# Lightning attention followed by a SiLU feed-forward layer on one core: four units as one group, scores ahead of outputs, and a new list

## The chip, the cores and the metric

The kernel runs on one core of a Trainium2 chip. The metric is device time in microseconds for one execution of the whole program. The core has five engines that run at the same time, each through its own list of instructions: PE (TensorE, the matmuls; its weight loads are shown apart as PEld), DVE (VectorE), ACT (ScalarE), POOL (GpSimd) and SP (SyncE, which here only issues DMAs). They wait for each other through semaphores. Matmuls read SBUF and write PSUM, which has eight banks of 128 partitions by 512 float32 values; DVE, ACT and POOL empty the banks.

## What is computed

```python
# q, k, v: 4 x 8 x 768 x 64 (batch, heads, positions, head size), lam: one rate per head; block = 64
for b in range(nb):                                    # 12 blocks in a row of the batch
    qb, kb, vb = (x[:, :, sl] for x in (q, k, v))      # sl: the 64 positions of block b
    intra = (einsum('bhic,bhjc->bhij', qb, kb) * Dmask) @ vb       # Dmask: lam ** (i - j), lower triangle
    inter = einsum('bhid,bhde->bhie', qb * lam_pow, kv_state)
    out[:, :, sl] = intra + inter
    kv_state = lam_block * kv_state + einsum('bhsd,bhse->bhde', kb * rev_pow, vb)
x = out.transpose(0, 2, 1, 3).reshape(3072, 512)       # 3072 tokens, 8 heads of 64
h = x @ w_in                                           # first product, 512 x 2048
return (h / (1 + exp(-h))) @ w_out                     # SiLU, second product, 2048 x 512
```

## The kernel before

**Tiles.** The 3072 tokens are cut into 24 *units* of 128. Two units form a *pair* (256 positions of one row of the batch); there are 12 pairs, three to a row. All matmuls run on bf16 operands and accumulate in PSUM.

**What happens to a pair n.** Its q, k and v are loaded (one DMA of 512 KB each on SP's queue), cast to bf16 and put in order (`cast`, L407 on ACT, L409 on DVE, L411 on POOL), v being multiplied by its decay at the same time (`scale`, L414, which gives `vd`). Keys and queries are then transposed into `kqT`: on TensorE for pairs 0 to 3, and by a transposing DMA on SP's queue for the others; there are three buffers `kqT`. Then comes the pair's *burst* on TensorE. From pair 3 on one burst holds, for the new pair n, the products that make the *states* (k against v, L659, 64 columns each) and the *scores* (k against q, L670, 128 columns each), and for the pair before, n-1, the *inter* products (the state against q, L633, which `CROSSED` pairs 4 to 11 use, and L617 for pair 3) and the *outputs* (masked scores against v, L626). Two half arrays of 64 rows are used, row 0 and row 1; the steps of a burst are made as two lists, one for each row, and these are merged by the time that each list has used so far. The order of the parts within a row is written out by hand at the end of `burst`. The inter products and the outputs of a unit accumulate into one bank; since both row halves of the array write there, a `fence` (an empty instruction on TensorE that waits for the last inter product) stands ahead of the first output.

After the burst DVE multiplies the scores by the triangle (`mask`, L414, giving `st`), and multiplies the outputs by their decay (`xt`, L414, 128x512 in bf16), which is the input of the first product. The states go through a chain: `y` (L789, DVE, the sum with the carried state), `xf` (L414, the decayed sum, on DVE or POOL), and two `xe` (copies to bf16 in `xs_all`, L407 or L411). The inter products of the next burst need these copies. So each burst waits for the masks and the copies of the pair ahead of it and for the transposed `kqT` of the new pair.

**First product** (`product1`, L935): x times w_in for a *group* of units, 16 slices of 128 columns of w_in by four slices of 128 rows. A group of two units has 256 columns for each matmul, a group of four has 512. ScalarE applies SiLU to each full bank (L951) and writes `g`. The groups of units 16 to 23 use a scheme of seven products in place of eight (`product1_of_four`, matmuls L1254) with sums of w_in and of x (`wsum`, `xsum`) and copies between the products (`to u`, `u2`, `u3`, and the sums `h22`, `h12`).

**Second product**: g times w_out. Units 0 to 11 take 16 matmuls of 512 columns each (`product2`, L977). The groups of units 12 to 23 take the scheme of seven products (`product2_of_four`, L1126). It needs sums of quarters of w_out (`bsum`, five of them, by m = 5, 1, 2, 7 and 6) and sums of g (`asum`). A sum is made by DVE or POOL (L1017), or by DMA: a copy on SP's queue and then an accumulating DMA on POOL's queue that adds the second operand. `MOVED` names the groups whose `asum` go by DMA (the lines L1107 and L1113 issue them), `BMOVED` the `bsum` that do.

**The opening** waits for the loads. TensorE runs filler matmuls on a tile of ones (L1321) until about 19 us. Each result goes out from `osb` by a DMA, mostly on ACT's queue.

**What sets the order.** All work is a list of tasks, each with a key (its due place), a cost on each engine that may take it, what it depends on, and the buffers that it holds. A list scheduler (`Planner.order`) plays the tasks through with these costs and pools of buffers (`POOLS`) and so fixes, before the program is built, on which engine and in which place of that engine's list every task stands. `SHIFT` adds to the key of named tasks, and `HOME` fixes the engine of named tasks. On the chip each engine runs its list in that order, so a task that is late holds up whatever stands behind it on its engine. `xt2` and `xt4` are the pools of `xt` for groups of two and of four units; eight banks are shared by all (four from the start, and the four of `st2` and `xd` once the first pairs are done).

Of the kernel before, what the change touches and what calls it, by code (L numbers as in the profile page):

```python
# [39 lines left out]
def names_of(tag):  # L40


    if not isinstance(tag, tuple):
        return tag, None, None
    kind, n = tag[:2]
    if kind in ("cast", "scale", "burst", "mask", "y", "xe", "xf", "xt"):
        whole = "pair", n
    elif kind in ("first", "silu", "x", "to u", "u2", "u3", "h12", "h22"):
        whole = "group", n
    elif kind in ("seven", "a", "a copy", "to P", "to B", "to R", "on R", "m3", "c11", "c12", "c21", "c22"):  # L50
        whole = "four", n
    else:
        whole = None
    return tag, tag[:2] if len(tag) > 2 else None, whole


class Planner:
# [5 lines left out]
    BEGIN = {"PE": 0.8, "ACT": 5.6, "DVE": 2.7, "POOL": 3.4, "SP": 0.8}  # L63
    SWITCH = 0.095

    SHIFT = {('cast', 10, 1, 0): -0.5, ('cast', 10, 1, 1): -2.5, ('cast', 6): -3.5, ('cast', 7, 1, 0): -1.5, ('first', 2): -0.5,
             ('first', 2, 6): -8, ('first', 3, 6): -8.5, ('first', 4, 4): 1, ('first', 5, 0): -4, ('first', 5, 6): -0.5,
             ('first', 6): 6.25, ('first', 6, 11): 2.25, ('first', 6, 12): -1, ('first', 6, 14): 13.25, ('first', 6, 15): 2.25,
             ('first', 6, 2): 0.5, ('first', 6, 3): 0.25, ('first', 6, 4): -4.5, ('first', 6, 5): -10.75, ('first', 7): -0.25,
             ('first', 7, 0, 4): 1.75, ('first', 7, 1, 4): 1, ('first', 7, 2, 3): 1, ('first', 8, 0, 5): -4,  # L70
             ('first', 8, 1, 1): -3.5, ('first', 8, 2, 4): 4.5, ('four', 12): 4.5, ('four', 20): -0.75, ('group', 2): 0.25,
             ('group', 3): -5.5, ('group', 7): 4.75, ('group', 8): -7.5, ('load w', 3, 1): -1.5, ('mask', 11): 5.75, ('mask', 5): 3,
             ('mask', 7, 0, 1): 3, ('mask', 8, 0, 0): 5.75, ('mask', 9, 0, 1): 0.25, ('outputs', 0, 0): 4, ('pair', 10): 2.5,
             ('pair', 11): -9.75, ('pair', 4): -7.5, ('pair', 5): -0.75, ('pair', 9): 8.75, ('scale', 3, 0): -1, ('score', 1): 8,
             ('second', 10): 7, ('seven', 12): 0.5, ('seven', 12, 3): -8.25, ('seven', 12, 5): -4.75, ('seven', 16): 3.75,
             ('seven', 20): 3.75, ('silu', 8, 1, 0, 1): 2.75, ('states', 2, 0): 6.75, ('store', 9): -2, ('turn', 3, 0, 1): -10.75,
             ('turned', 1): -7.25, ('u3', 8): 5.5, ('w', 1): 6.75, ('xe', 0, 0, 1): 4.5, ('xe', 11): 11.75, ('xe', 3, 0, 0): 1.5,
             ('xf', 6): -10.25, ('xt', 7, 1): 7, ('y', 10, 0, 0): 5.75}
    HOME = {('a', 16, 1, 1): 'POOL', ('a', 20, 5, 0): 'POOL', ('a', 20, 5, 1): 'POOL', ('b', 3, 1): 'POOL',
            ('cast', 11, 1, 1): 'POOL', ('cast', 3, 0, 1): 'ACT', ('cast', 4, 0, 0): 'DVE', ('cast', 5, 0, 0): 'POOL',  # L80
            ('cast', 5, 1, 0): 'POOL', ('cast', 5, 1, 1): 'ACT', ('cast', 6, 0, 0): 'DVE', ('cast', 6, 1, 0): 'DVE',
            ('cast', 6, 1, 1): 'ACT', ('cast', 7, 1, 0): 'DVE', ('cast', 7, 1, 1): 'ACT', ('cast', 8, 1, 1): 'DVE',
            ('cast', 9, 0, 0): 'POOL', ('cast', 9, 1, 0): 'POOL', ('cast o', 1, 1): 'DVE', ('cast o', 2, 0): 'ACT',
            ('cast o', 2, 1): 'ACT', ('cast w', 1, 3): 'POOL', ('m3', 12): 'DVE', ('result', 1): 'ACT', ('scale', 11, 0): 'POOL',
            ('scale', 9, 0): 'POOL', ('to u', 7, 3): 'DVE', ('turned', 0, 0, 1): 'DVE', ('turned', 0, 1, 0): 'ACT',
# [3 lines left out]
    FIRST, LAST, AHEAD = {"SP": 1.15, "ACT": 1.15, "POOL": 1.0}, 1.0, 0.75  # L89

    def __init__(self, pools, becomes):
# [194 lines left out]
def kernel(  # L286
# [15 lines left out]
    NU = B * S // U  # L302
    NP = H // 2
# [3 lines left out]
    EARLY = 4  # L307
    FINE = (0,)
    TIED, SOLO, CROSSED = 3, (3,), range(4, 12)
    AWAY, XAWAY, OWN = range(5,12), (), (0, 1)  # L310
    PORT = 3
    SMALL = (0, 1)
    OKEY = 0.0
    WKEY, WCAST, WON = -2.0, {"POOL": 0.75, "ACT": 0.62, "DVE": 0.45}, [("POOL", "ACT", "DVE")] * 2 + [("POOL", "DVE"), ("POOL", "ACT")]
    FIRST_ONES, ONES_UNTIL = 10, 19.0
    BMOVED, POOLED = (), (6,)
    LOADED, MOVED, HEAD = (4, 9), (12,16), (1.8, 1.8, 1.2, 0.6)
    TKEY, SEVENS, LAG, WSKEY, FIRST_SEVENS = 9.0, 12, 5.0, 14.0, (16,20)

    ctx.enter_context(tc.manual_schedule())  # L320
    const = ctx.enter_context(tc.tile_pool(name="const", bufs=1))
# [281 lines left out]
    def burst(n, alone=False):  # L603
# [3 lines left out]
        o, new = dict(last_pair), n < NU // 2 and not alone  # L607
# [38 lines left out]
        if new:  # L646
            kq, kqT, vd, ck, cv, turned, kq_of, t_of = ready_of[n]
# [28 lines left out]
        def queue(row, what, width, fn, *more, part=slice(None)):  # L676
            rows[row].extend([(what, 0.0005 + 0.00044 * width, lambda a=(k, r) + more: fn(*a), k) for k, r in steps][part])
# [52 lines left out]
    def attention(n):  # L730
# [593 lines left out]
    ends, first = {}, {}  # L1324
# [61 lines left out]
```

## Time and profile before

| | before |
|---|---|
| three runs, us | 204.65, 205.16, 205.41 (median 205.16) |
| the profiled execution, us | 204.5 |
| its span, first to last instruction, us | 202.8 |
| granted TensorE clock, share of full speed | 0.998 |
| bytes moved by DMA | 44.43 MB, mean 219 GB/s |

All times are those of one core. The profile is one execution; `span` runs from its first to its last instruction, and the rest of its own time lies around that. A busy share is the time that an engine worked over the span. In the rows of a view, a line such as `PE banks L935 x40` is a run of 40 instructions of line 935 on TensorE that write `banks`; `out<-in` gives the tiles with their partitions by elements and type, and `x16` a count. In the timeline the first column is the start in us from the span's start and the second how long the run of instructions lasted until the last of them ended. Matmuls overlap: the next one starts before the last has ended, so for a pace one takes the distance of starts. The list of waits has rows `waiting <- released by: us, times, longest`. The rows of DMA queues give issues, KB each and the median us from issue to landing; those of issuing instructions give the least, the median and the longest issue in ns.

### The profile page before, as it was taken

The page shows a single profiled execution, that of the slowest core. Times are in us where ns is not written, and L with a number is a line of the kernel's source. Part 1 is how long each engine was busy: PE and PEld are TensorE (multiplying, and loading weights), DVE is VectorE, ACT ScalarE, POOL GpSimd, SP SyncE. Part 2 cuts the span into 40 slices and gives each one's busy share as a digit, 9 for nine tenths or more (in the row PEclk, how much of TensorE's full clock was granted, in tenths as well). Part 3 has the DMA queues.
Part 4 walks back from the last instruction along what each step waited for, and adds up shares of the span by engine and source line. Part 5 has one row for each costly group of instructions (what it writes and reads, how often), then busy time and mean ns, then how long its engine had stood idle before and what let it go on. Part 6 is the DMA issues. An engine that isn't in the chain of part 4 may idle for free.

```text
span 202.8 us, 6082 instructions
## 1 busy us (share of the span) xinstructions
PE 196.8 (97%) x2585; PEld 145.3 (72%) x2585; DVE 146.2 (72%) x231; ACT 123.4 (61%) x193; POOL 71.4 (35%) x84
## 2 busy tenths in 40 slices
PE   6999999999999999999999999999999999999993
PEld 2776887867865557557776465458888888888882
DVE  3697749778994949599795875969765766743972
ACT  3697887849785655705384626683796878564010
POOL 4105430222560400058766041338954372000800
PEclk9999999999999999999999999999999999999999
DMA  4999999999999999899999471119997967111324
GB/s 110 339 335 366 386 362 334 368 313 382 230 282 261 318 344 298 208 311 218 303 255 213 130 128 33 57 58 222 176 184 184 218 179 136 52 55 52 107 103 155
DMA packets 71658, 44.43 MB, mean 219 GB/s; under 512 B 18448, under 2 KB 64528, under 8 KB 71632
## 3 DMA queue, kind: packets, MB, share of 16 engines
q1 hardware_dynamic: 62400, 34.74, 62.4%
q0 software_dynamic: 5456, 4.46, 14.4%
q10 hardware_dynamic: 3776, 4.86, 7.2%
q8 instruction: 20, 0.33, 0.6%
q14 instruction: 6, 0.05, 0.1%
HBM read 27.27 MB, written 6.29 MB: 165 GB/s over the span
## 4 chain that ended last, share of the span: by engine, by line
PE 90%; DVE 5%; issue 2%; ACT 1%; ACTq 0%
PE banks L935 27%; PE banks L1126 18%; PE banks L977 17%; PE banks L1254 12%; PE banks L1321 4%; PE banks L626 2%; PE banks L670 2%; PE banks L578 2%; DVE kq L409 1%; DVE xt L414 1%; PE banks L633 1%; DVE st L414 1%; PE banks L659 1%; PE banks L848 1%; PE banks L898 1%
## 5 line engine op out<-in xcount | busy, mean ns | idle before, releaser
L935 PE MATMUL banks<-xt,w_in_bf 128*128 128x256 bf16 (+1 forms) x448 | 67.4, 288 | 0.4 <-DVE xt L414 0.2
L951 ACT ACTIVATE g<-banks 128x512 bf16<-128x512 f32 x64 | 46.0, 745 | 26.8 <-PE banks L935 25.4
L935 PEld LDWEIGHTS <-w_in_bf 128*128 128x128 bf16 x448 | 42.9, 98 | 15.3 <-issue 0.8
L977 PE MATMUL banks<-w_out_bf,g 128*128 128x512 bf16 x192 | 49.6, 379 | 0.0
L414 DVE TENSOR_TENSOR st<-banks,tri 128x512 bf16<-128x512 f32 (+1 forms) x42 | 29.9, 757 | 3.7 <-PE banks L670 2.9
L977 PEld LDWEIGHTS <-g 128*128 128x128 bf16 x192 | 18.3, 98 | 19.1
L414 DVE TENSOR_TENSOR xt<-banks,lam_xe 128x512 bf16<-128x512 f32 x24 | 16.0, 684 | 12.5 <-PE banks L626 12.3
L1126 PE MATMUL banks<-bsum,g 128*128 128x256 bf16 x160 | 21.2, 273 | 0.0
L407 ACT ACTIVATE kq<-raw 64x512 bf16<-64x512 f32 (+3 forms) x24 | 18.5, 799 | 2.7 <-DMA raw<-in_k_dram 1.2
L407 ACT ACTIVATE osb<-banks 128x512 f32<-128x512 f32 (+1 forms) x15 | 8.7, 582 | 17.5 <-PE banks L977 12.2
L1126 PEld LDWEIGHTS <-asum 128*128 128x128 bf16 x176 | 17.2, 98 | 2.0
L409 DVE CAST kq<-raw 64x512 bf16<-64x512 f32 (+3 forms) x21 | 15.2, 741 | 4.0 <-DMA raw<-in_k_dram 2.5
L1126 PEld LDWEIGHTS <-g 128*128 128x128 bf16 x160 | 15.6, 98 | 1.9
L414 POOL TENSOR_TENSOR xf<-y,lam_be 128x256 f32<-128x256 f32 (+1 forms) x11 | 8.2, 749 | 22.1 <-DVE y L789 21.9
L1017 DVE TENSOR_TENSOR asum<-g 128x1024 bf16<-128x1024 bf16 x11 | 9.1, 836 | 8.3 <-PE banks L1126 2.9
L1270 ACT ACTIVATE g<-tmp 128x512 bf16<-128x512 f32 x16 | 12.4, 774 | 3.5 <-DVE tmp L1017 3.3
L1017 DVE TENSOR_TENSOR tmp<-banks,tmp 128x512 f32<-128x512 f32 x16 | 11.0, 687 | 4.8 <-PE banks L1254 4.1
L414 DVE TENSOR_TENSOR vd<-raw,lam_v 128x1024 bf16<-128x1024 f32 (+1 forms) x11 | 12.3, 1120 | 3.0 <-DMA raw<-in_v_dram 2.9
L1254 PE MATMUL banks<-xsum,wsum 128*128 128x256 bf16 x96 | 14.4, 273 | 0.0
L1017 POOL TENSOR_TENSOR asum<-g 128x1024 bf16<-128x1024 bf16 x3 | 6.4, 2121 | 22.8 <-PE banks L1126 19.1
L1254 PEld LDWEIGHTS <-wsum 128*128 128x128 bf16 x128 | 12.4, 98 | 1.5
L1321 PE MATMUL banks<-ones 128*128 128x128 bf16 (+1 forms) x85 | 11.0, 277 | 1.9 <-DVE ones L358 1.5
(96 smaller groups left out, 294.6 us busy)
## 6 DMA issues: line engine op xcount, KB each, us to landing
raw<-in_k_dram SPq DMA_DIRECT2D x11, 512.0 KB, 5.4
raw<-in_q_dram SPq DMA_DIRECT2D x11, 512.0 KB, 6.1
raw<-in_v_dram SPq DMA_DIRECT2D x11, 512.0 KB, 7.6
out_dram<-osb ACTq DMA_DIRECT2D x18, 256.0 KB, 3.6
raw_w<-in_moe_w_in_dram SPq DMA_DIRECT2D x8, 512.0 KB, 8.0
raw_w<-in_moe_w_out_dram SPq DMA_DIRECT2D x8, 512.0 KB, 6.6
asum<-g SPq DMA_DIRECT2D x8, 256.0 KB, 2.6
asum<-g POOLq DMA_DIRECT2D x8, 256.0 KB, 5.1
```

Of the source, the lines that this page charges most:

```text
L407: nc.scalar.activation(o, i, AF.Copy)
L409: nc.vector.tensor_copy(o, i)
L414: (nc.vector if e == "DVE" else nc.gpsimd).tensor_tensor(o, a, b, op=AL.mult)
L578: nc.tensor.transpose(t[:, r, m, :], kq_of()[:, i, r, 2 * m:2 * m + 2, :], ident)
L935: nc.tensor.matmul(t[:, j, :], lhsT=w_in_bf[:, ko, 128 * m:128 * m + 128], rhs=xt[gi].tile[:, ko, :], start=(ko == 0), stop=(ko == KI - 1))
L951: nc.scalar.activation(t.rearrange("p j (c a r) -> p (j c) r a", c=n // U, r=2), psum_of(bank).rearrange("p (jc r a) -> p jc r a", r=2, a= ...
L977: nc.tensor.matmul(psum_of(bank), lhsT=gs[gi, ko][1](1, 128 * gp, 128)[:, 0], rhs=w_out_bf[:, ko], start=(ko == 0), stop=(ko == KO - 1))
L1017: (nc.vector if e == "DVE" else nc.gpsimd).tensor_tensor(o, x, y, op=op)
L1126: nc.tensor.matmul(part(bank, u), lhsT=lhs(u), rhs=b_of(ko), stop=ko == 7, skip_group_check=True, start=opens and not ko and not u)
L1254: nc.tensor.matmul(two_of(bank)[:, f], lhsT=(wb[0].tile if wb else w_quarter(*wl))[:, ko, fs], rhs=(xsum(xr) if isinstance(xr, int) else x ...
L1270: nc.scalar.activation(t.rearrange("p j (c a r) -> p (j c) r a", c=2, r=2), src().rearrange("p (jc r a) -> p jc r a", r=2, a=64), AF.Silu)
L1321: nc.tensor.matmul((t if b.pool == "bank" else t[:, 0])[:, 0:w], lhsT=ones[:, 0:128], rhs=ones[:, 0:w], start=True, stop=True)
```

## The change

Four things are changed. (1) Units 8 to 11 form one group of four where they were two groups of two, and the pools of `xt` go from four and two buffers to two and three. (2) In a burst of a new pair that also holds the outputs of a pair in `CROSSED` (4 to 11), row 0 gets two steps of scores ahead of its outputs (it had none) and row 1 six (it had four); the rest of the scores still follow the outputs. A step is two matmuls. (3) The sums of w_out with m = 1, 7 and 6 go by DMA (`BMOVED`). (4) `SHIFT` and `HOME` are replaced as a whole, so that the scheduler gives a new list. In `SHIFT`, `HOME` and the spelling of four lines nothing else is touched.

```diff
-    SHIFT = {('cast', 10, 1, 0): -0.5, ('cast', 10, 1, 1): -2.5, ('cast', 6): -3.5, ('cast', 7, 1, 0): -1.5, ('first', 2): -0.5,
...
-            ('xf', 10, 0, 1): 'POOL', ('xf', 4, 0, 1): 'DVE', ('xf', 7, 0, 0): 'POOL'}
+    SHIFT = {('cast', 11, 1, 0): -0.5, ('cast', 5, 0, 1): 2, ('cast', 7, 1, 0): 7, ('cast o', 2, 0): -5, ('first', 2, 3): 1.5,
...
+             ('xe', 9, 0, 0): -3, ('xf', 6): -1.5, ('y', 10, 0, 0): -3.5, ('y', 6): -2.5, ('y', 8, 0, 0): -2}
+    HOME = {('a', 20, 2, 1): 'POOL', ('b', 4, 0): 'POOL', ('cast', 10, 1, 0): 'DVE', ('cast', 11, 0, 0): 'ACT',
...
+            ('xe', 6, 0, 0): 'POOL'}
...
-    BMOVED, POOLED = (), (6,)
+    BMOVED, POOLED = (1, 7, 6), (6,)
...
-                 xt2=4, xt4=2, g=7, osb=4, one=3, two=2, set=2)
+                 xt2=2, xt4=3, g=7, osb=4, one=3, two=2, set=2)
...
-    groups = [[0, 1], [2, 3], [4, 5], [6, 7], [8, 9], [10, 11]] + [list(range(4 * n, 4 * n + 4)) for n in range(3, NU // 4)]
+    groups = [[0, 1], [2, 3], [4, 5], [6, 7], ] + [list(range(4 * n, 4 * n + 4)) for n in range(2, NU // 4)]
...
-            ahead = NP if new and o["n"] in CROSSED else 0
+            ahead = (2, NP + 2) if new and o["n"] in CROSSED else (0, 0)
             if new:
-                queue(1, "s", 128, score, 1, part=slice(ahead))
+                queue(0, "s", 128, score, 0, part=slice(ahead[0]))
+                queue(1, "s", 128, score, 1, part=slice(ahead[1]))
             queue(0, "o", 128, output, 0)
             queue(1, "o", 128, output, 1)
...
-            queue(0, "s", 128, score, 0)
+            queue(0, "s", 128, score, 0, part=slice(ahead[0] if o else 0, None))
             if o:
-                queue(1, "s", 128, score, 1, part=slice(ahead, None))
+                queue(1, "s", 128, score, 1, part=slice(ahead[1], None))
```

The code that `BMOVED` chooses is in the kernel before as well; for a sum named there it issues the copy on SP and the addition on POOL:

```python
t = add((TKEY + i / 4 - 2, 0), {"SP": 0.55}, put, deps=deps[0] + deps[1], bufs=[b], tag=("b copy", m), prior=loaded[0],
        nbytes=0.524, kind=WIDE)
ts = [add((TKEY + i / 4, 0), {"POOL": 2.9}, more, deps=[t], bufs=[b], tag=("b", m, 0), nbytes=0.524, kind=WIDE)] * 2
```

More of the change, by code (lines that the diff above doesn't have):

```diff
@@ L64 @@
     SWITCH = 0.095
-    SHIFT = {('cast', 10, 1, 0): -0.5, ('cast', 10, 1, 1): -2.5, ('cast', 6): -3.5, ('cast', 7, 1, 0): -1.5, ('first', 2): -0.5,
[L67 to L85, printed above, removed]
[3 rows of a table removed]
+    SHIFT = {('cast', 11, 1, 0): -0.5, ('cast', 5, 0, 1): 2, ('cast', 7, 1, 0): 7, ('cast o', 2, 0): -5, ('first', 2, 3): 1.5,
+             ('first', 2, 5): 3, ('first', 2, 7): 1.75, ('first', 5): 3.25, ('first', 5, 10): 6.25, ('first', 5, 12): 6,
+             ('first', 5, 13): 10.25, ('first', 5, 15): 7, ('first', 5, 8): 3, ('first', 6): 7, ('first', 6, 0, 5): -3.75,
+             ('first', 6, 1, 2): -0.25, ('first', 6, 1, 5): 5.5, ('first', 6, 2, 1): 1.25, ('first', 6, 2, 2): 4,
+             ('first', 6, 2, 3): 7, ('first', 6, 3, 4): 0.25, ('first', 6, 3, 7): 5.5, ('first', 7, 0, 7): 1.5,
+             ('first', 7, 1, 2): -6.75, ('four', 20): 2.5, ('group', 5): -6, ('group', 6): 0.5, ('inter', 2, 0): 9.75,
+             ('load w', 3, 1): -1.5, ('pair', 10): -7.25, ('pair', 4): 0.25, ('pair', 5): -6, ('pair', 7): -9, ('pair', 9): -8.5,
+             ('result', 1): -0.5, ('scale', 3, 0): -1, ('scale', 8): -5.5, ('second', 0): 2.25, ('seven', 12, 1): 10.5,
+             ('seven', 16): 13.25, ('seven', 16, 6): 5.25, ('seven', 20): 14, ('store', 9): -2, ('to u', 7, 1): 0.5,
+             ('turn', 1, 0, 0): -4.75, ('turned', 1, 0, 1): 5, ('turned', 2): 8.25, ('xe', 0, 0, 1): 4.5, ('xe', 3, 0, 0): 1.5,
+             ('xe', 9, 0, 0): -3, ('xf', 6): -1.5, ('y', 10, 0, 0): -3.5, ('y', 6): -2.5, ('y', 8, 0, 0): -2}
@@ new lines @@
+    HOME = {('a', 20, 2, 1): 'POOL', ('b', 4, 0): 'POOL', ('cast', 10, 1, 0): 'DVE', ('cast', 11, 0, 0): 'ACT',
+            ('cast', 11, 0, 1): 'DVE', ('cast', 11, 1, 0): 'ACT', ('cast', 11, 1, 1): 'DVE', ('cast', 3, 0, 1): 'ACT',
+            ('cast', 4, 0, 0): 'ACT', ('cast', 4, 0, 1): 'DVE', ('cast', 5, 0, 0): 'POOL', ('cast', 5, 1, 0): 'ACT',
+            ('cast', 7, 1, 0): 'DVE', ('cast', 8, 0, 0): 'POOL', ('cast', 8, 1, 0): 'POOL', ('cast', 9, 0, 0): 'POOL',
+            ('cast', 9, 1, 0): 'POOL', ('cast o', 2, 0): 'DVE', ('cast o', 3, 1): 'DVE', ('cast o', 3, 3): 'DVE',
+            ('cast w', 1, 3): 'POOL', ('result', 1): 'ACT', ('scale', 10, 0): 'POOL', ('to P', 12): 'ACT', ('to u', 7, 1): 'ACT',
+            ('turned', 0, 1, 0): 'ACT', ('turned', 2, 0, 0): 'DVE', ('turned', 2, 0, 1): 'ACT', ('u3', 6, 0): 'ACT',
+            ('u3', 7, 2): 'DVE', ('w', 3, 0): 'POOL', ('x', 6, 4): 'POOL', ('x', 7, 2): 'POOL', ('xe', 4, 0, 0): 'DVE',
+            ('xe', 6, 0, 0): 'POOL'}
@@ L309 @@
     TIED, SOLO, CROSSED = 3, (3,), range(4, 12)
-    AWAY, XAWAY, OWN = range(5,12), (), (0, 1)
+    AWAY, XAWAY, OWN = range(5, 12), (), (0, 1)
     PORT = 3
@@ L315 @@
     FIRST_ONES, ONES_UNTIL = 10, 19.0
-    BMOVED, POOLED = (), (6,)
-    LOADED, MOVED, HEAD = (4, 9), (12,16), (1.8, 1.8, 1.2, 0.6)
-    TKEY, SEVENS, LAG, WSKEY, FIRST_SEVENS = 9.0, 12, 5.0, 14.0, (16,20)
+    BMOVED, POOLED = (1, 7, 6), (6,)
+    LOADED, MOVED, HEAD = (4, 9), (12, 16), (1.8, 1.8, 1.2, 0.6)
+    TKEY, SEVENS, LAG, WSKEY, FIRST_SEVENS = 9.0, 12, 5.0, 14.0, (16, 20)
     ctx.enter_context(tc.manual_schedule())
```

2 rows, old and new, of the table HOME are left out of this document.

## The prediction

> **What bounds the kernel now.** I read the page's busy shares first, then the list of who waited for whom on TensorE, then the chain of work that ended last.
>
> ```profile
> span 202.8 us, 6082 instructions
> PE 196.8 (97%) x2585; PEld 145.3 (72%) x2585; DVE 146.2 (72%) x231; ACT 123.4 (61%) x193; POOL 71.4 (35%) x84
> ```
>
> ```profile
> PE banks L1321 <- DVE ones L358: 1.5, 1, 1.5
> PE banks L1321 <- DVE st L414: 0.3, 1, 0.3
> PE banks L935 <- DVE xt L414: 0.2, 1, 0.2
> PE banks L898 <- PE banks L879: 0.2, 1, 0.2
> PE banks L626 <- PE banks L633: 0.2, 1, 0.2
> ```
>
> A share of 97% alone proves little, since the ends of matmuls are modelled. The five waits say more: these are all of TensorE's idle stretches, 2.4 us together, and 1.8 us of them stand before the filler matmuls (L1321) of the opening. Shorter holes do not appear there; I find them from starts below. So from the first product to the end the time is the sum of TensorE's own work. The opening and the tail stand outside that sum:
>
> ```profile
> 15.86 1.85 POOL L411 CAST w_in_bf<-raw_w 128x512 bf16<-128x512 f32 x3 [1.83 <-DMA raw_w<-in_moe_w_in_dram]
> ```
>
> ```profile
> 50.64 1.75 PE banks L935 x16
> ...
> 120.05 3.45 PE banks L935 x16
> ...
> 126.84 8.74 PE banks L935 x40
> ...
> 178.06 21.63 PE banks L1126 x198
> 199.76 0.38 ACT osb L407
> ```
>
> The opening ends when the first quarter of w_in has landed and is cast; the new list leaves the first 36 entries of SP's load queue as they were, so I move nothing there. From 178.06 TensorE runs without a break to the final copy at 199.76 and the last store; the last products and the tail keep their shape. What is left to gain is work taken from TensorE, or holes closed, between about 17.5 and 199.7 us.
>
> **The change, part by part.**
>
> *Units 8 to 11 as one group.* 128 matmuls of 256 columns become 64 of 512. From the rows above, 256 columns take 1.75/16 = 0.109 us from start to start and 512 take 3.45/16 = 0.216 (0.2185 over the stretch of 40, which begins behind a burst). Two narrow ones cost 0.219, so each merged pair saves between 0.000 and 0.003 us: 64 of them 0 to 0.2 us. I take 0.13. The same number of SiLUs of 128x512 remains on ScalarE.
>
> *Two more steps of scores ahead, per row.* Here the burst is read by starts. This is burst 6 in the timeline of TensorE, and below it pieces of the chain for bursts 5, 10, 11 and 12:
>
> ```profile
> 87.28 0.42 PE L633 MATMUL banks<-kqT,xs_all 64*64 64x128 bf16 x16
> 87.53 0.19 PE L659 MATMUL banks<-vd,kq 64*64 64x64 bf16 x2
> ...
> 87.89 0.64 PE L626 MATMUL banks<-st,vd 64*64 64x128 bf16 x32
> 88.33 0.22 PE L659 MATMUL banks<-vd,kq 64*64 64x64 bf16 x3
> ...
> 88.58 0.42 PE L670 MATMUL banks<-kqT 64*64 64x128 bf16 x16
> ```
>
> ```profile
> 74.96 0.56 PE banks L626 x32
> ...
> 125.82 0.54 PE banks L626 x30
> ...
> 126.61 0.23 PE banks L670 x16
> ...
> 136.17 0.56 PE banks L626 x32
> ...
> 143.61 0.38 PE banks L633 x16
> 143.99 0.14 issue
> 144.13 0.64 PE banks L626 x32
> ```
>
> Between the 16 inter products (L633) and the outputs (L626) stand 16 state and 8 score matmuls, 87.53 to 87.89 = 0.36 us. The same 24 after the outputs go from 88.33 to 88.58 = 0.25. The missing 0.11 us is the fence: the outputs write the bank of the inter products and wait until these are through. Bursts 5, 10 and 11 agree: 0.54 for 30 and 0.56 for 32 outputs, where 32 at the pace of L670 (0.23/16) take 0.46. Burst 12, which has no scores to put there, waits longest (0.14 beside 0.38 for the same 16). The change moves 2 x 2 steps, 8 score matmuls, from behind the outputs to before them: 8 x 0.0144 = 0.115 us of work that is there anyway, about what the wait lasts. It applies where the earlier pair is 4 or later and a new pair comes in: bursts 5 to 11, seven of them. Saving: between 0 (if the wait moves along) and 7 x 0.115 = 0.8 us; I take 7 x 0.11 = 0.77, since a fence asks for a fixed time after the last inter product, and the order only decides what runs meanwhile. The scores need no input that the burst has not already waited for.
>
> *The list in new order.* It keeps all other TensorE work: I counted the same matmuls of every other kind (288 outputs, 288 scores, 192 of the second product, 336 and 224 of the two seven-product schemes), with five more fillers in the opening, where loads decide. What can change are holes. The one worth naming lies behind burst 6:
>
> ```profile
> 88.93 1.90 PE L977 MATMUL banks<-w_out_bf,g 128*128 128x512 bf16 x8
> 91.05 3.05 PE L935 MATMUL banks<-xt,w_in_bf 128*128 128x256 bf16 x24 [0.22 <-DVE xt L414]
> 93.94 1.03 PE L977 MATMUL banks<-w_out_bf,g 128*128 128x512 bf16 x4
> ```
>
> ```profile
> 86.32 3.95 DVE L409 CAST kq<-raw 64x1024 bf16<-64x1024 f32 x3
> 90.30 0.69 DVE L414 TENSOR_TENSOR xt<-banks,lam_xe 128x512 bf16<-128x512 f32 x1
> ```
>
> Eight of the second product fill 8 x 0.216 = 1.73 us, to 90.66, but the next starts at 91.05: 0.39. Its 24 fill 2.62 us, to 93.67, then 93.94: 0.27. Both wait for VectorE to empty a bank (xt), which came late behind three casts of 3.95 us. In the new order two half casts and a scale stand between the masks of burst 5 and xt, and seven second products (1.51 us) plus the rest of the burst (0.6 us) cover the two xt (1.4 us). So 0.66 us can go; but the first product of units 8 to 11 now needs the xt of both pairs, so the same lateness would stall there again. Bounds: 0.66 gained, or with the same late casts and less cover 0.66 lost. I take half the gain, 0.33.
>
> *Sums of w_out moved to DMA.* Three of five sums leave VectorE (rows below, six halves of about 1.1 us) and become a copy on SP and an accumulating DMA on POOL, 512 KB each.
>
> ```profile
> L1017 DVE TENSOR_TENSOR bsum<-w_out_bf 128x1024 bf16<-128x1024 bf16 x9 | 9.2, 1081 | 0.0
> ...
> L414 POOL TENSOR_TENSOR xf<-y,lam_be 128x256 f32<-128x256 f32 x9 | 7.2, 796 | 12.3 <-DVE y L789 12.1 <-PE banks L935 0.3
> ...
> L411 POOL CAST xs_all<-xf 64x256 bf16<-64x256 f32 x4 | 1.7, 413 | 3.5 <-DVE xf L414 3.4
> ```
>
> ```profile
> L1113 POOL DMA_DIRECT2D asum<-g x8: 848/1308/2873, 137.9 to 166.8; - x8
> L1113 POOL DMA_DIRECT2D g<-g x8: 1155/1448/3967, 141.0 to 167.3; - x8
> ```
>
> ```profile
> asum<-g SPq DMA_DIRECT2D x8, 256.0 KB, 2.6
> asum<-g POOLq DMA_DIRECT2D x8, 256.0 KB, 5.1
> ...
> kqT<-kq SPq DMA_TRANSPOSE x8, 6.6
> ```
>
> VectorE's 6.6 us were off TensorE's path (TensorE did not wait at 52 to 72 us), so they give nothing directly. The sums are first used in the second product of units 12 to 15, after burst 12, and their issues stand before burst 11 in POOL's queue, over 20 us ahead. What hides them is that distance; what is queued behind them is the xf and the two xe of pair 10, which burst 11 needs. On SP the last two copies stand ahead of the last transpose; that one must wait for burst 9 to free its buffer anyway, and at 6.6 us it lands some 5 us before burst 11. Cost taken: 0; the dear end is the third rival. POOL's issues here took between 0.85 and 3.97 us for 256 KB, so their length is not fixed. The Trainium skill (DMA: Bandwidth & Descriptors, SWDGE vs HWDGE vs iDMA) says that GpSimd writes its descriptors into SBUF and is locked out while VectorE runs in its two-port mode, which DMAs from SP are immune to; this spread fits that, but no row here separates it. By the medians the sum stays as it is; by that rule the issues lengthen under VectorE's casts, and the time is that of the third rival.
>
> **Sum.** 0.13 + 0.77 + 0.33 = 1.23 us less. The profiled execution took 204.5 us (span 202.8 and 1.7 around it), so it would take 203.3; the median of the runs, 205.16, is 0.66 above it and gives 203.9.
>
> **The rivals.**
>
> 1. *The small gains go into new short waits.* The new list brings the product groups of units 12 to 23 behind others: between their seven products stand copies of about 0.6 to 0.7 us (for xt of that size the row reads 0.69) with 1.1 to 1.3 us of matmuls to hide copy and latency. Before, TensorE met no hole over 0.15 us there; eight such places with 0.1 to 0.2 us each would cost 0.8 to 1.6 and give 204.7 to 205.5. For it: there is little slack per place. Against: the old list was as tight and ran dry nowhere. Chance 0.25.
>
> 2. *The fence does not get shorter*: the 0.11 us is a price of turning to the outputs, and moves with them. Then 205.16 - 0.13 - 0.33 = 204.7. Against it: coming back from outputs to states at 88.33 costs nothing (32 outputs in 0.44 us), and burst 12, with nothing put between, waits longer. Chance 0.08.
>
> 3. *Burst 11 waits for POOL; slower.* In the new order burst 11 starts 36 second and 48 first products of 0.216 us and three bursts of 1.6 us after burst 8: 22.9 us (burst 10 to 11: 7.0, before 136.17 - 125.82 = 10.4 between their outputs). The copies of the last two sums go out behind the transpose that waits for a buffer of burst 8, which by the order and the same paces is about 4.6 us later, and land up to 2 x 2.6 us after that, at some 10 us. Two accumulating issues follow, then xf and two xe, 0.80 + 2 x 0.41 = 1.6 us. It decides once an issue takes more than (22.9 - 10 - 1.6)/2 = 5.6 us. By the medians it is 2 x 1.31 to 2 x 1.45 = 2.6 to 2.9; by the longest, 7.9, the stall is 2 x (7.9 - 5.6) = 4.6 us: 205.16 - 1.23 + 4.6 = 208.5. For it: the spread of the issues, and a burst 3 us nearer to its predecessor. Against: the medians leave half the time free. Chance 0.15.
>
> **How the numbers follow.** The forecast holds 0.52; its own range is 203.2 (all 0.66 gained, 0.2 for the merge, and the runs' own scatter) to 204.6 (0.66 lost again with most of the rest kept, 205.16 - 0.13 - 0.77 + 0.33). About 0.5%, 1.0 us, is what a measurement of this kernel can tell from no change: 204.1 and below counts as faster, above 206.2 as slower. The forecast lies only 0.2 us beyond the first bound. Of its 0.52 I put 0.42 below it and 0.10 between; rival 1 gives 0.06 faster (waits nearer to nothing), 0.16 same and 0.03 slower; rival 2 gives 0.02 and 0.06; rival 3 gives 0.02 same and 0.13 slower. Together 0.50 faster, 0.34 same, 0.16 slower. The range of 203.0 to 206.8 leaves out the far end of rival 3 and a little below.
>
> **What would show it.** In the new profile: in bursts 5 to 11 the states and scores between inter products and outputs last 0.36 to 0.40 us with a third more matmuls, and 32 outputs cost 0.46 in the chain; the list of TensorE's waits has no xt entry and nothing over 0.3 us after 18 us; burst 10 to 11 is 7.0 us apart; POOL's three long issues end before y of pair 10. I am wrong if TensorE waits for POOL's xs_all or xf before burst 11, for xt before the first product of units 8 to 11, or for copies between the seven products by more than 1 us in all, or if the holes in the bursts stay at 0.11.

## The result, and the profile after

| | before | after |
|---|---|---|
| median of six runs, us | 204.94 | 203.57 |
| ratio, 95% interval | | 0.9943, 0.993 to 0.9956 |
| the profiled execution, us | 204.5 | 203.53 |
| its span, us | 202.8 | 201.6 |

The changed kernel is faster by 0.57% (0.44 to 0.70). By the medians that is 1.37 us, by the ratio 1.17. The medians are those of all six runs; the ratio leaves out one run of after, 206.96 us at a granted clock of 0.992. The prediction was 203.9 on 205.16, that is 1.23 us or 0.60% less. In the profiled executions the span became 1.2 us shorter. Line numbers of after lie two or three lower than before: L630 are the inter products, L656 the states, L667 the scores, L623 the outputs, L933 the first product, L975 the second, L1124 and L1252 the seven products of either.

The page of after, its first lines; then all rows of what TensorE waited for (waiting <- released by: us in total, times, longest):

```profile
span 201.6 us, 5956 instructions
PE 195.3 (97%) x2526; PEld 138.2 (69%) x2526; DVE 142.3 (71%) x235; ACT 122.3 (61%) x189; POOL 68.2 (34%) x81
```

```profile
PE banks L1319 <- DVE ones L355: 1.5, 1, 1.5
PE banks L933 <- ACT w_in_bf L404: 0.4, 1, 0.4
PE banks L933 <- POOL w_in_bf L408: 0.4, 1, 0.4
PE banks L623 <- PE banks L630: 0.2, 1, 0.2
```

The share of busy time is 97% as before and tells nothing. The row of L935 waiting for xt is gone, and behind the opening (its two w_in rows are waits for the casts of w_in, the later one ending at 18.17 us) only burst 12's fence is left.

The chain of waits of after (start, us, what), at burst 5, behind burst 6, at the starts of bursts 10 and 11, and at the end:

```profile
74.26 0.35 PE banks L630 x16
...
74.79 0.03 PE banks L667
74.86 0.11 PE banks L667 x8
74.97 0.45 PE banks L623 x31
...
84.71 1.62 PE banks L975 x7
86.33 9.50 PE banks L933 x44
...
123.73 0.23 PE banks L630 x3
...
130.73 0.35 PE banks L630 x16
...
175.90 22.29 PE banks L1124 x204
198.20 0.38 ACT osb L404
```

Burst 5: eight scores now stand right ahead of the outputs, and 31 outputs take 0.45 us, the pace of a score; before, 32 took 0.56. Behind burst 6 the seven second products last 1.62 us up to 86.33, and 44 first products follow at once, 9.50/44 = 0.216 us each. The two holes of 0.39 and 0.27 us are closed. The final copy starts at 198.20 where it started at 199.76, 1.56 us earlier; the span shrank by 1.2 only, so the tail behind the copy has grown from 3.04 to 3.40 us.

VectorE in the timeline of after, at the xt of pair 5, and POOL ahead of burst 11 (which starts at 130.73 in the chain):

```profile
84.40 1.29 DVE L411 TENSOR_TENSOR xt<-banks,lam_xe 128x512 bf16<-128x512 f32 x2 [2.02 <-PE banks L623]
```

```profile
120.86 1.53 POOL L1051 DMA_DIRECT2D bsum<-w_out_bf  x1 [7.48 <-DVE xt L411]
123.69 1.53 POOL L1051 DMA_DIRECT2D bsum<-w_out_bf  x1 [1.30 <-DVE vd L411]
126.69 0.61 POOL L411 TENSOR_TENSOR xf<-y,lam_be 128x256 f32<-128x256 f32 x1 [1.46 <-DVE y L787]
127.36 0.83 POOL L408 CAST xs_all<-xf 64x256 bf16<-64x256 f32 x2
```

Before the xt, VectorE now stands idle for 2.02 us and waits for the outputs; before the change it was the late one. POOL is done with both issues at 125.22 and then waits 1.46 us for y; its copies end at 128.19, 2.5 us ahead of burst 11.

### The profile page after: what moved, and what is told of

It reads as the page before. It is cut to its first block, busy times and chain, and to the rows that moved or that the text cites. A ratio compares the mean times of both kernels' runs of the same rounds, so it can differ in the third digit from the quotient of the medians.

```text
span 201.6 us, 5956 instructions
## 1 busy us (share of the span) xinstructions
PE 195.3 (97%) x2526; PEld 138.2 (69%) x2526; DVE 142.3 (71%) x235; ACT 122.3 (61%) x189; POOL 68.2 (34%) x81
## 4 chain that ended last, share of the span: by engine, by line
PE 89%; SPq 5%; DMA 3%; ACT 1%; issue 0%
PE banks L933 28%; PE banks L975 21%; PE banks L1124 18%; PE banks L1252 12%; SPq L429 4%; DMA raw_w<-in_moe_w_in_dram 3%; PE banks L667 2%; PE banks L623 2%; PE banks L630 1%; PE banks L656 1%; PE banks L575 1%; SPq L448 1%; PE banks L896 1%; PE banks L846 1%; PE banks L877 0%
## 5 line engine op out<-in xcount | busy, mean ns | idle before, releaser
L933 PE MATMUL banks<-xt,w_in_bf 128*128 128x256 bf16 (+1 forms) x384 | 64.2, 308 | 0.7 <-ACT w_in_bf L404 0.4
L949 ACT ACTIVATE g<-banks 128x512 bf16<-128x512 f32 x64 | 46.3, 744 | 18.5 <-PE banks L933 15.7
L933 PEld LDWEIGHTS <-w_in_bf 128*128 128x128 bf16 x384 | 36.7, 98 | 20.4 <-ACT w_in_bf L404 0.6
L975 PE MATMUL banks<-w_out_bf,g 128*128 128x512 bf16 x192 | 47.7, 379 | 0.0
L975 PEld LDWEIGHTS <-g 128*128 128x128 bf16 x192 | 18.2, 98 | 19.8
L408 POOL CAST kq<-raw 64x512 bf16<-64x512 f32 (+1 forms) x16 | 15.0, 961 | 18.1 <-DMA raw<-in_q_dram 16.1
L404 ACT ACTIVATE kq<-raw 64x1024 bf16<-64x1024 f32 (+2 forms) x21 | 18.1, 883 | 2.5 <-DMA raw<-in_v_dram 1.5
L1124 PE MATMUL banks<-bsum,g 128*128 128x256 bf16 x160 | 19.4, 273 | 0.0
L1124 PEld LDWEIGHTS <-asum 128*128 128x128 bf16 x176 | 17.2, 98 | 2.0
L1124 PEld LDWEIGHTS <-g 128*128 128x128 bf16 x160 | 15.7, 98 | 1.8
L1111 POOL DMA_DIRECT2D asum<-g x8 | 9.9, 1281 | 17.8 <-DMA asum<-g 11.0
L1268 ACT ACTIVATE g<-banks 128x512 bf16<-128x512 f32 x16 | 11.6, 741 | 4.5 <-PE banks L1252 4.3
L1252 PE MATMUL banks<-xsum,wsum 128*128 128x256 bf16 x96 | 14.2, 273 | 0.0
L1252 PEld LDWEIGHTS <-wsum 128*128 128x128 bf16 x128 | 12.4, 98 | 1.7
L411 POOL TENSOR_TENSOR xf<-y,lam_be 128x256 f32<-128x256 f32 (+1 forms) x6 | 4.9, 811 | 22.9 <-DVE y L787 16.9
L406 DVE CAST kq<-raw 64x512 bf16<-64x512 f32 (+3 forms) x21 | 10.3, 512 | 2.9 <-DMA raw<-in_k_dram 2.5
```

The source lines that it names most:

```text
L404: nc.scalar.activation(o, i, AF.Copy)
L406: nc.vector.tensor_copy(o, i)
L408: nc.gpsimd.tensor_copy(o, i)
L411: (nc.vector if e == "DVE" else nc.gpsimd).tensor_tensor(o, a, b, op=AL.mult)
L933: nc.tensor.matmul(t[:, j, :], lhsT=w_in_bf[:, ko, 128 * m:128 * m + 128], rhs=xt[gi].tile[:, ko, :], start=(ko == 0), stop=(ko == KI - 1))
L949: nc.scalar.activation(t.rearrange("p j (c a r) -> p (j c) r a", c=n // U, r=2), psum_of(bank).rearrange("p (jc r a) -> p jc r a", r=2, a= ...
```

## The experiments

Three theories stood against each other: the gain is the fence that is covered (0.77) and the late xt (0.33 to 0.66); it comes from the merged group or the moved sums; or from the new list as a whole. To tell them apart, several kernels keep the list of one of the two kernels exactly and change only what is issued inside it. Times are medians beside runs of the kernel before on the same chip (204.88 to 204.96).

**The new order of the bursts, on the old list.** The scheduler still reckons with the old order, and the bursts issue the new one:

```diff
+    PLANNED, ISSUED = (0, NP), (2, NP + 2)
...
+        (plan_order, plan_cuts), (order, cuts) = merged(PLANNED), merged(ISSUED)
...
-                ts.append(add((2 * n - 8.5 - alone, j), {"PE": order[cut - 1][3] - spent}, go,
+                ts.append(add((2 * n - 8.5 - alone, j), {"PE": plan_order[cut - 1][3] - spent}, go,
```

(`merged` is the loop that builds and merges the two rows, with the number of scores ahead as its argument.)

> The kernel before with nothing changed but the order inside the bursts of pairs 5 to 11: two steps of scores ahead in row 0 and six in row 1. The lists of all other engines and the order of TensorE's other work are kept as they were. Theory (the fence asks for a fixed time after the last inter product, and 8 more score matmuls cover it): in each of the seven bursts the extra step between states and outputs, 95 to 134 ns over the pace in the kernel before, goes to under 30 ns; 0.75 us in all, 204.94 - 0.75 = 204.2. Rival (the step is a price of turning to the outputs and moves along): the extra steps stay at 0.09 to 0.13 us and the time at 204.9.

Measured: 204.11, ratio 0.9966 (0.9945 to 0.9986), 0.77 us less by the medians and 0.70 by the ratio (0.29 to 1.13). Its chain at burst 5:

```profile
74.62 0.35 PE banks L634 x16
...
75.21 0.11 PE banks L671 x8
75.33 0.45 PE banks L627 x31
```

0.45 us for 31 outputs, as in after: this part alone brings the covered fence, without any other edit.

**Half the dose:** `ISSUED = (0, NP + 2)` in the same kernel.

> As the run before, but with half the dose: no step ahead in row 0 and six in row 1, so 4 more score matmuls (0.058 us) in place of 8 ahead of the outputs. Theory (a fixed time after the last inter product): each extra step shrinks by 0.058 us, to 40 to 75 ns; 7 x 0.058 = 0.4 us in all, 204.5. Rival (a price of turning): 204.9 and steps as before. Second rival (any row-0 work in front is what matters, not its length): no change here, the whole 0.75 in the run before.

Measured: 204.56, ratio 0.9982 (0.9967 to 0.9998). The time fits 0.4 less (the interval is 0.04 to 0.68), but the steps do not: the chain shows why.

```profile
75.36 0.04 PE banks L671 x2
75.40 0.13 PE banks L627 x2
75.53 0.01 PE banks L671 x2
75.53 0.39 PE banks L627 x28
75.92 0.05 PE banks L671 x2
```

The first two outputs still take 0.13 us. The rows are merged by time used; row 0 has no scores ahead, so its first output, with the fence in front, comes after two of the four extra scores, and the rest stand behind the wait. What counts is how much work stands ahead of the first output of *either* row, so the two steps that the change gives row 0 are needed as well. The expectation of 0.058 us for each burst was wrong for this reason: from first inter product to last score, by the starts of the matmuls, the seven bursts together got 0.15 us shorter here and 0.78 us with the full dose.

**Still more ahead, on the new list:** `PLANNED, ISSUED = (2, NP + 2), (4, NP + 4)`.

> The kernel after with still more ahead in bursts 5 to 11: four steps of scores in row 0 and all eight in row 1. Theory (a fixed time of 0.38 us, which two steps cover but for 10 to 30 ns): the step from the last score to the first output goes to nothing, the bursts get shorter by 0.1 to 0.2 us in all, and the rest only changes places: 203.4 to 203.6. Rival (each score taken ahead saves its own time): as much again as the first two steps, 202.8.

Measured: 203.49, ratio 0.9941 (0.9911 to 0.9972): the same as after. In the chain of its burst 5 the outputs take what they took:

```profile
74.98 0.23 PE banks L668 x16
75.20 0.45 PE banks L624 x32
```

So a score taken ahead saves nothing of its own. Here the first output of burst 5 starts 0.50 us after the last inter product, behind 40 matmuls; in after it is 0.39 behind 32. With 40 the work fills the time, and no wait is left to cover. The profiled execution has something else, in burst 11:

```profile
131.60 0.22 PE banks L624 x16
131.83 0.94 issue
132.77 0.42 PE banks L624 x16
```

In the middle of the outputs TensorE stood for 0.94 us and waited for nothing that the trace shows. What causes it stays open. One lead: in this trace the DMA queue that carries instructions (q8 on the page) moves a packet of 16 KB at 130.50 us, in after at 128.01, ahead of the same burst; that TensorE stood for it is not shown.

**The old order of the bursts, on the new list:** `PLANNED, ISSUED = (2, NP + 2), (0, NP)`; once alone and once with after beside it on the same chip.

> The kernel after with the old order inside bursts 5 to 11 (no step of scores ahead in row 0, four in row 1); every list and all else as after. Theory: the fixed time of the fence (370 to 410 ns from the last inter product to the first output in every burst seen so far) comes back into view, 7 x 0.11 = 0.77 us: 203.57 + 0.77 = 204.3. Rival (the new list and not the order brings the gain, and the two overlap): 203.6 to 203.8.

> The kernel after, unchanged, for a comparison on one chip with the two beside it: 203.6 as before, with bursts 5 to 11 as in its first profile.

> The kernel after with the old order inside bursts 5 to 11, a second time, now beside after on the same chip. Theory: the bursts are 0.11 us longer each, as in its first trace, and the time is 0.5 to 0.9 us above that of after. Rival (waiting elsewhere takes most of it, so that the order is worth less in the new list than in the old): 0.2 to 0.4 above.

Measured: alone 203.90 (ratio 0.9953, 0.9935 to 0.9971); side by side 204.45 (0.9968, 0.9946 to 0.9991), and after 203.33 (0.9927, 0.9908 to 0.9947). The run alone, 0.3 above the earlier median of after, pointed to the rival; side by side it is 1.1, and by the ratios 0.0041 x 205 = 0.84. The intervals are some 0.8 us across each, and 0.77 lies between the two answers. The traces are plainer: by the starts of the matmuls the seven bursts together are 0.78 us longer with the old order than in after.

**One instruction of POOL moved, on the old list.** Behind the planning, POOL's half sum of w_in goes further back in POOL's list, ahead of an instruction that starts at 117.06; in the trace it runs at 110.69 us where it ran at 87.50, so 23 us later and not 30:

```diff
     planned = plan.order()
+    late = next(x for x in planned if x[3].tag == ("w", 3, 0))
+    planned.remove(late)
+    at = next(i for i, x in enumerate(planned) if x[2] == "POOL" and x[3].tag == ("scale", 11, 0))
+    planned.insert(at, late)
```

> The kernel before with one instruction moved: POOL's half sum of w_in (128x1024, 2.14 us, at 87.5 us) stands some 30 us later in POOL's list, where it is still 20 us ahead of its first use; nothing else is moved. Theory (the holes of 0.38 and 0.28 us behind burst 6 come from VectorE's cast of 64x512, which took 2.92 us while POOL worked on that sum, and 0.42 us elsewhere): the cast takes about 0.42, the xt of pair 5 come 2.5 us earlier, both holes close, 204.94 - 0.65 = 204.3. Rival (the cast is slow by itself, or the late xt has another cause): the cast stays near 2.9 us and the time at 204.9.

Measured: 204.02, ratio 0.9966 (0.9943 to 0.9989), 0.86 less by the medians and 0.70 by the ratio (0.23 to 1.17). First two rows of the kernel before, VectorE's casts as a group (least, median and longest in ns) and POOL beside them, then VectorE's timeline and TensorE's chain of this one:

```profile
L409 DVE CAST kq<-raw x3: 418/675/2922, 86.3 to 89.9; 64x512 bf16<-64x512 f32 x2, 64x1024 bf16<-64x1024 f32 x1
```

```profile
87.50 2.14 POOL L1017 TENSOR_TENSOR wsum<-w_in_bf 128x1024 bf16<-128x1024 bf16 x1
```

```profile
86.20 1.46 DVE L409 CAST kq<-raw 64x1024 bf16<-64x1024 f32 x3
88.45 0.69 DVE L414 TENSOR_TENSOR xt<-banks,lam_xe 128x512 bf16<-128x512 f32 x1 [0.80 <-PE banks L626]
```

```profile
88.88 1.83 PE banks L977 x8
90.71 2.62 PE banks L935 x24
93.33 0.86 PE banks L977 x4
```

The three casts take 1.46 us in place of 3.95, xt starts at 88.45 in place of 90.30, and the second and first products follow each other without a hole. The cause of the late xt was one cast of 2.92 us that took 0.42 without POOL's sum beside it. The collision is moved and not removed: at its new place POOL's sum (110.69 to 112.81) stands beside a product of 64x256 on VectorE that takes 1.68 us, 0.42 elsewhere. In after it is a sum of VectorE from 90.13 that takes 3.02 us, 1.10 elsewhere, beside POOL's sum from 90.48 to 92.59. In neither list does TensorE wait for what stands behind.

**Both of these edits on the old list, and nothing else** (the first diff and this last one together):

> The kernel before with two edits alone: the new order inside bursts 5 to 11, and POOL's half sum of w_in moved 30 us later in POOL's list. No merged group, no sums by DMA, no other move. Theory (these two are the gain of the whole change, but for 0.13 us of the merge): 204.9 - 0.77 - 0.65 = 203.5, as fast as after within 0.2. Rival (merge, DMA sums or other moves in the list carry part of the gain): 204.0 or more.

Measured: 203.44, ratio 0.9921 (0.9899 to 0.9943). The whole change has 0.9943 and 0.9927. So two local edits carry all of the gain that can be measured; the merged group, the sums by DMA and the rest of the new list add nothing beyond the interval, which is some 0.9 us across.

**The group alone.** The kernel before with units 8 to 11 as one group, its tables kept and the list planned anew:

```diff
-    groups = [[0, 1], [2, 3], [4, 5], [6, 7], [8, 9], [10, 11]] + [list(range(4 * n, 4 * n + 4)) for n in range(3, NU // 4)]
+    groups = [[0, 1], [2, 3], [4, 5], [6, 7], ] + [list(range(4 * n, 4 * n + 4)) for n in range(2, NU // 4)]
...
-                 xt2=4, xt4=2, g=7, osb=4, one=3, two=2, set=2)
+                 xt2=2, xt4=3, g=7, osb=4, one=3, two=2, set=2)
```

> The kernel before with units 8 to 11 as one group (and the pools of xt that go with it); its own tables of shifts and homes, with the group numbers behind it counted one lower; the scheduler is run anew. Theory (the merge saves 0 to 0.2 us by the paces and asks for the late xt of both pairs at once): 64 matmuls of 512 columns at 0.216 us, 0.13 us less of TensorE's own work; what the holes behind burst 6 do with old tables is open, 0.66 us at most either way: 204.2 to 205.5. Rival (the merge itself brings most of the gain of the change): 203.9 or less with the fence steps still there.

Measured: 207.06, ratio 1.011 (1.0082 to 1.0138): 2.2 us slower, outside what was expected. Two waits of TensorE are new:

```profile
PE banks L1126 <- DMA asum<-g: 1.1, 2, 0.8
PE banks L977 <- ACT w_out_bf L407: 0.5, 1, 0.5
```

Neither is at the group, and together they are 1.6 us of the 2.2. Tables that were made for one list did not fit this one; the merge itself, 0 to 0.2 us by the paces, can't be seen under that. This run tells what a new list may cost, not what the merge costs.

**The sums of w_out back on the engines, new list:** `BMOVED = ()`; some ten other instructions move with it.

> The kernel after with no sum of w_out moved to DMA, as in the kernel before; the scheduler puts the six half sums on VectorE or POOL and moves some ten other instructions. Theory (the sums are hidden in either place, as the prediction's zero says): 203.4 to 203.9, no new wait of TensorE. Rival (VectorE needs the time that the DMAs freed, so that an xt or a copy comes late): waits of TensorE for VectorE of 0.5 us or more, 204.1 or above.

Measured: 203.76, ratio 0.9932 (0.9907 to 0.9957), the same as after beside it. Its waits have one row that is longer than in after, at the start of the first product, and none for xt or a copy:

```profile
PE banks L933 <- POOL w_in_bf L408: 0.7, 1, 0.7
```

That wait moves from execution to execution with the loads of the opening (0.4 in the first trace of after). A further row that the first trace of after lacks, six stretches of 0.2 us ahead of L975 for which no releaser is given, stands in the trace of after beside this one as well: both traces hold 181 of the 192 matmuls of L975, and a missing record looks like a hole. The sums are hidden in either place, as far as intervals of 0.8 to 1.0 us can tell.

**The accumulating DMAs in eight parts each, new list:**

```diff
-                    nc.gpsimd.dma_start(out=b.tile, in_=b_quarter(*qs[1]), accum_op=AL.add)
+                    for ko in range(0, 8, 1):
+                        nc.gpsimd.dma_start(out=b.tile[:, ko:ko + 1], in_=b_quarter(*qs[1])[:, ko:ko + 1], accum_op=AL.add)
```

> The kernel after, but each of the three accumulating DMAs of the sums of w_out is issued as eight of an eighth each, in the same place of POOL's list. In the profile of after the second and the third issue start at 120.86 and 123.69 us and take 1.5 each, xf of pair 10 follows at 126.69 and its two copies end at 128.19, 2.1 us ahead of burst 11; so this costs nothing until one sum's issues take over 4 us together. If an issue costs about the same whatever its size (0.76 us, the least on POOL): 6.1 us for each sum, the last ends at 133.1, burst 11 starts 4.2 us late, and the time is 207.7, with TensorE waiting for xs_all ahead of burst 11. If it goes by bytes: 1.5 us for each sum, 203.6.

Measured: 213.13, ratio 1.0362 (1.0314 to 1.0409). The profiled execution is the longest of its runs, 219.07. What TensorE waited for there, and POOL's issues (least, median, longest in ns):

```profile
PE banks L630 <- POOL xs_all L408: 12.8, 1, 12.8
```

```profile
L1052 POOL DMA_DIRECT2D bsum<-w_out_bf x24: 854/1571/3638, 116.0 to 138.2; - x24
```

Below are POOL's timeline at the first eight, and the granted clock of TensorE in 40 equal slices of the span (5.4 us each), in tenths:

```profile
115.98 7.10 POOL L1052 DMA_DIRECT2D bsum<-w_out_bf  x8 [5.02 <-DMA bsum<-w_out_bf]
```

```profile
PEclk9999999999999999999999999557999999999999
```

The place is the one that was named: burst 11 waits for xs_all behind POOL's issues. The price was more than twice what was expected (9.6 us above the 203.57 of after, where 4.1 was expected), and the trace shows three reasons. In a row an issue took 0.89 us (7.10 for eight) where 0.76 was taken; the records are longer than that because those of a row overlap. POOL also stood 4.4 us between the issues for DMAs to land. And after TensorE's wait of 12.8 us its granted clock was 0.50 up to 149.1 us: until then matmuls of 512 columns started 0.427 us apart and not 0.216. A part of 64 KB cost at least 0.85 us to issue, where 512 KB cost 1.53: an issue goes by the piece far more than by bytes.

**The last store on the last semaphore, new list.** Five small loads in an idle stretch of SP's queue:

```diff
+        if e == "SP" and isinstance(t.tag, tuple) and t.tag[0] == "a copy":
+            for i in range(more):
+                nc.sync.dma_start(out=pad[:, 8 * i:8 * i + 8], in_=w_in_r[:, 0, 8 * i:8 * i + 8])
+            more = 0
```

> The kernel after with five small loads (128 x 8 floats each, into a tile that nothing reads) on SP's queue, in a stretch in which SP has nothing to do (121.6 to 134 us); all other lists as after. At its end the program's SP waits in turn for each of eight semaphores of DMA queues, about 0.06 us each; in the kernel before the last store uses the last of the eight, in the kernel after the third, and five waits follow it (the end of the span comes 0.92 us behind the last landing before, 1.22 after). With five DMAs more the last store uses the last semaphore again. Theory (these five waits are the 0.3 us that the tail of after is longer): last landing to the end 0.92 us, 203.3 to 203.6 less 0.3: 203.0 to 203.3. Rival (the tail is longer by what the new list leaves in flight): 1.2 us as in after, 203.3 to 203.6.

Measured: 203.88, ratio 0.9948 (0.9919 to 0.9978). SP's semaphore events from the last landing to the end, in before, in after and in this kernel:

```profile
L1381 SPq EVENT_SEMAPHORE  x3: 17/17/28, 201.9 to 202.7; - x3
```

```profile
L1379 SPq EVENT_SEMAPHORE  x8: 17/28/28, 200.4 to 201.5; - x8
```

```profile
L1383 SPq EVENT_SEMAPHORE  x3: 17/17/28, 201.1 to 201.9; - x3
```

Eight became three again, and the closing is 0.3 us shorter (0.92 us from the last landing to the end, 1.22 in after), as the theory says. The median did not follow: five runs lie at 203.00 to 203.27, where the theory put them, the others at 203.75 and above. In the profiled execution burst 10 took 0.76 us longer than in after, by the starts of its matmuls. The loads themselves did that, as the list of TensorE's waits and the chain show (L667 are the scores):

```profile
PE banks L667 <- ACT g L949: 0.4, 2, 0.2
```

```profile
112.33 9.55 DMA bsum<-w_out_bf
121.97 0.34 ACTq L962
122.41 0.16 ACT g L949
...
123.60 1.22 ACT g L949 x2
124.85 0.31 PE banks L667 x8
```

The DMAs of SP and ACT use the eight semaphores in turn, and an issue waits until the DMA before it on its semaphore has landed. With five loads more, ScalarE's store of a result (L962) stands five places on, on the semaphore of a copy for a sum of w_out that lands at 121.89. ScalarE was done with the copy into `osb` at 119.03 and issued the store at 121.97; in after it did so 0.03 us behind that copy, on a semaphore that had been free since 109.66. The SiLUs (L949) behind the store came late, and with them the banks for the scores. So the tail is explained; this version is not faster than after by its time, and its edit did more than it was meant to.

## Why the prediction was right, point by point

- **What bounds the kernel.** TensorE's own stream, as stated: the gain came from two kinds of holes in it, and of the unloaded VectorE, the moved sums and the merged group none shows in the time.
- **The fence, 0.77.** Right in mechanism and size. The wait ran out a fixed time after the last inter product, and the scores that were there anyway filled it. Alone it measured 204.88 - 204.11 = 0.77 (0.70 by the ratio), and taken out of the new list 0.3 and 1.1; by the starts of the matmuls it is 0.78 in either list. It does not scale with the number of scores: half the dose gave far less than half of the gain in the steps, and a double dose nothing more.
- **The merge, 0.13.** Its pace is as forecast (9.50/44 = 0.216 us against 2 x 1.75/16 = 0.219). The runs can't resolve it.
- **The hole behind burst 6, 0.33.** The mechanism was right, the size was half. Both holes, 0.66 us together, closed. The prediction kept half back in case the late xt would meet the merged group; but it had not asked why three casts took 3.95 us, and so missed that one of them was held up by POOL's sum, which the new list puts elsewhere, at 90.48. The upper end of the forecast's own range, 204.6, adds 0.33 where the bound that it names is 0.66 lost; with that it would have been 204.9.
- **"The last products and the tail keep their shape."** This step was wrong by 0.3 us. SP's closing waits come behind the last store, and which semaphore that store uses depends on how many DMAs went before. By the terms: 0.13 + 0.77 + 0.66 less 0.3 is 1.26, with the 0.13 as forecast; the span shrank by 1.2. The two errors, 0.33 too little and 0.3 too much, cancel; that the total is closer than its terms is luck.
- **The moved sums, 0.** Right as far as the runs can tell: 203.76 without them against 203.33 with, with intervals of 0.8 to 1.0 us.
- **Rival 1** (short waits between the seven products) did not come: the list of waits has none there. **Rival 2** (the fence does not get shorter) fell with the first experiment. **Rival 3** (POOL's issues hold up burst 11) is a real mechanism and lay far from its threshold: POOL had 1.46 us before xf and 2.5 behind its copies. Its breakeven was put too high, though. By the starts of after, two issues from 120.86, then 1.44 us for xf and its copies, with burst 11 at 130.73, leave (130.73 - 120.86 - 1.44)/2 = 4.2 us each and not 5.6, since the copies landed later than reckoned: at 120.23 and 123.16, 12.5 and 15.4 us after the start of burst 8, and not at some 10. The dear end of the rival was misread as well. In the kernel before, the six issues in a row from 137.87 start 0.74 to 0.85 us apart while their records grow from 1.33 to 3.97 us, so the records overlap; the six took 7.82 us, 1.30 each, and the longest record is not the price of one issue; nor does this spread show that VectorE locks POOL out. An issue of 512 KB took 1.53 to 1.62 us, where 2.6 to 2.9 was reckoned from those of 256 KB.
- **The signs.** Bursts 10 and 11 start 7.0 us apart (123.73 and 130.73 in the chain), no xt stands among the waits, and POOL's issues end before y of pair 10, all as forecast. One sign is missed by a little: a wait of 0.4 us for a cast of w_in ends at 18.17, and nothing over 0.3 was to stand after 18.

## What to carry to other kernels

On an engine that is busy 97% of the time, look for holes between starts and ask of each what it waits for by name: here two kinds of holes, 0.77 and 0.66 us in all, were the whole gain that can be measured, and each kind could be closed by an edit to one place. A fixed wait is covered by putting work that exists anyway in front of it, in every row that feeds the instruction that waits; more than the wait cost nothing and saved nothing here. Where an instruction takes several times its usual time, look at what the other engines do in that stretch before taking its duration as its price. The same holds for records in a row: by the distance of their starts one sees whether they overlap.

## What the runs showed of the hardware that was not expected

- VectorE's cast of 64x512 from float32 to bf16 took 2.92 us while POOL added two bf16 tiles of 128x1024 (2.14 us), and 0.42 alone. The Trainium skill (SBUF — State Buffer, section "Who interferes with whom") says that VectorE in its two-port modes and GpSimd share a port pair, that whoever comes first holds it for the whole instruction, and that the other blocks. The trace agrees that the two hold each other up: moving POOL's addition away took the three casts from 3.95 to 1.46 us. It does not bear out who comes first: by the records the cast began at 87.01, 0.48 us ahead of POOL's addition, and yet ended 0.30 us behind it. Why that is stays open.
- From the start of the last inter product to that of the first output it was 0.37 to 0.41 us in bursts 5 to 11 of before and of after, with 24 matmuls between them or with 32, and 0.38 in burst 12, where nothing stands between. With 40 it was 0.50 in burst 5, which is the matmuls' own time.
- At the end of the program SP waits for eight DMA semaphores in turn, about 0.06 us each. The last store uses the third of them in after and the last in before, and 0.3 us more of such waits follow it in after.
- The DMAs of SP and ACT share these eight semaphores in turn. Five small loads in a queue with nothing to do held up a store of ScalarE for 2.9 us, since it came to stand on the semaphore of a copy that had not landed.
- TensorE stood for 12.8 us in the run with issues in eight parts, and the granted clock was then 0.50 for the first 5.5 us of work: matmuls of 512 columns started 0.427 us apart and not 0.216.
- In one trace of these runs (still more ahead, burst 11) TensorE stood for 0.94 us in the middle of a run of 64x64 matmuls with no wait in the trace. That is more than any one hole that the change closes, and its cause was not found.
